# Linear attention into an MLP mixer: the first batch's steps in another order, with other PSUM banks

## The chip, the cores and the metric

The kernel runs on one core of a Trainium2 chip. The metric is device microseconds (us) of one execution. The kernel before took 245.57 us, the median of three runs (244.58 to 246.3). Lower is better.

## The reference

Inputs are q, k and v in float32, each of 8 batches x 8 heads x 576 positions x 64, and four weight matrices. Per batch:

```
phi(x) = where(x > 0, x, exp(x) - 1) + 1
kv  = phi(k)^T v                 # 64 x 64 per head
z   = sum over positions of phi(k)
x   = (phi(q) kv) / (phi(q) z + 1e-6)      # 576 x 512, heads side by side
u   = x + (relu(x^T w_tok1) w_tok2)^T      # token mixing, 576 -> 256 -> 576
out = u + relu(u w_ch1) w_ch2              # channel mixing, 512 -> 1536 -> 512
```

The output is 8 x 576 x 512 in float32.

## The kernel before

Matmuls run in bfloat16 and gather in float32 in PSUM, which has eight banks of 128 x 512. The 576 positions of a batch are cut into four full row blocks of 128 and a half one of 64 (the code's R = 4 and the index r = R); two batches share one block of tails. The eight batches go through the same stages, overlapped: loads, phi, kv, numerators and denominators, token mixing, channel mixing. Batches 1 to 7 do the channel mixing's products by a Winograd scheme with weight sums in place; batch 0 multiplies plainly.

**Order by hand.** Every step of the kernel is a named token (`put(name, fn)`), and the string `ORDER` lists all 1085 tokens; line 1167 emits them in that sequence. Each engine runs its own instructions strictly in that sequence, so `ORDER` is the queue of TensorE (PE), VectorE (DVE), ScalarE (ACT), GpSimd (POOL) and of the loads on SyncE (SP) at once. `BANK` gives each PSUM tile its bank by name, `EBUF` gives each exponential one of three SBUF buffers. A step waits for whoever wrote its inputs and for whoever still reads the bank or buffer it overwrites.

**The names that matter.** The leading digit is the batch. Batch 0's attention and token mixing are the tokens `A0` to `A43`, in the list `first` (line 1144):

- `A0`, `A4`, `A8`, `A16`: exponentials of k and q, in halves c = 0 and 1, on ACT (line 252); `A1`, `A5`, `A9`, `A17` (line 256) and `A3`, `A6`, `A11`, `A21` (line 262) finish phi on DVE.
- `A2`, `A14`, `A19`: `warm`, matmuls of zeros whose results nobody reads (line 1092).
- `A7`, `A15`: q turned by PE (line 320); `A10`, `A12`, `A18`, `A22`: the copies out of PSUM, on DVE or ACT (line 326).
- `A13`, `A25`: `ksum_first`, the sums z (line 564), with two small ACT copies (line 567). `A20`, `A26`: `kv_first` (line 573), with two ACT copies (line 577).
- `A23`, `A29`: denominators and numerators of a half (lines 588 and 595). `A24`, `A30`: reciprocals, `A27`, `A33`, `A35`: quotients, on DVE (lines 604 to 610). `A28`, `A31`: quotients of the half block, on ACT (line 619).
- `A32`, `A34`, `A36`, `A37`: `mm1_first`, the first token-mixing matmuls (line 627) with a relu on ACT (line 630). `A38`, `A39`, `A40`, `A43`: `mm2_first` (line 638), each with an add into u on DVE (line 640). `0gt`, `0gv`: the same for the half block (lines 653 and 658). `A41`, `A42`, `At2`, `At3`: u turned by PE (line 646) and copied out by ACT or DVE (line 648).

Then come, for batch 0, `0ma`/`0mb` 0 to 11: the first channel-mixing matmuls, in two halves of the contraction (line 686), with relus `0r` on ACT (line 695) or, for 3, 6 and 9, on DVE (line 693); and `0q0` to `0q11`, the second ones (line 747). For batch 1: loads `1L` (line 228), phi `1kx 1ka 1kb 1qx 1qa 1qb`, `1v0` (DVE) and `1v1` (ACT), which cast v (line 275), `1Q` and `1Qc` (lines 320, 326), `1K` and `1Kc` (lines 302, 308), numerators `1n` with `1nc` on DVE (lines 352, 361 to 364), `1f` with `1fr` on ACT (lines 448, 452), `1h` with `1hu` (lines 520, 523, 531, 533) and `1t` (line 538). `G..` are weight sums on DVE (line 897), `wt2` another (line 824), `ws..` weight sums on POOL (line 816). `B0` to `B2` load the last three quarters of w_ch2 (line 1126).

**Gates.** Three waits between transfers are written out: the load `1Lk0` waits until the first quarter of w_ch1 has landed, `B0` waits until the second half of batch 1's v (`1Lv1`) has landed, and `2Lq0` waits until the second quarter of w_ch2 (`B0`) has landed. The transfer `1Lq0`, half of batch 1's q, is issued fourth in SP's row of batch 1.

**The copies of w_tok2.** `w2_put` (line 664) sorts w_tok2's columns into `w2p`, which `mm2_first` reads: four copies, by kt = 0, 1 and by columns t = 0 to 3 and 4 to 8. They stand ahead of `ORDER`, all four on POOL.

Of the kernel before, what the change touches and what calls it, by code (L numbers as in the profile page):

```python
# [24 lines left out]

GSW = {2: 0, 1: 1, 0: 2}
# [15 lines left out]
BANK = {k_: int(v_) for k_, v_ in (e.split(":") for e in """2K:0 2n0:0 2n1:2 2n2:4 2f:6 2g0:3 2g1:6 2X2:5 2Z2:2 2Y2:1 2gt:6 3K:6 3n0:2 3n1:4 3n2:6 3f:3 3g0:6 3g1:6 3X2:2  # L42
3Z2:0 3Y2:5 3gt:4 4K:2 4n0:2 4n1:4 4n2:6 4f:6 4g0:4 4g1:0 4X2:2 4Z2:1 4Y2:3 4gt:6 5K:6 5n0:1 5n1:3 5n2:5 5f:5
5g0:5 5g1:3 5X2:4 5Z2:5 5Y2:7 5gt:1 6K:2 6n0:1 6n1:3 6n2:5 6f:2 6g0:5 6g1:2 6X2:4 6Z2:0 6Y2:6 6gt:6 7K:2 7n0:2
7n1:4 7n2:6 7f:2 7g0:0 7g1:2 7X2:3 7Z2:6 7Y2:1 7gt:5 2m2:0 2m3:1 2m4:2 2m5:3 2m8:1 2m9:1 2m10:0 2m11:1 3m2:0
3m3:1 3m4:2 3m5:3 3m8:1 3m9:0 3m10:0 3m11:1 4m2:0 4m3:1 4m4:2 4m5:3 4m8:1 4m9:1 4m10:0 4m11:1 5m2:0 5m3:1
5m4:2 5m5:3 5m8:1 5m9:0 5m10:0 5m11:1 6m2:0 6m3:1 6m4:2 6m5:3 6m8:1 6m9:1 6m10:0 6m11:1 1h00:7 1h01:6 1h10:5
1h11:6 1t0:7 1t1:0 1t2:1 1t3:6 1m0:2 1m1:0 1m2:0 1m3:4 1m4:5 1m5:6 1m6:6 1m7:2 1m8:5 1m9:7 1m10:1 1m11:6 T00:7
T10:3 T01:3 T11:0 T02:3 T12:7 U08:0 U18:3 7c0:3 7c1:4 7c2:4 7c3:6 7c4:2 7c5:4 7X0:5 7Z0:4 7Y0:1 7X1:2 7Z1:0
7Y1:0 7PX0:7 7PZ0:3 7PY0:1 7PX1:6 7PZ1:5 7PY1:5 7tX:0 7tZ:4 7tY:2 1PX:1 1PZ:2 1PY:5 2PX:0 2PZ:5 2PY:1 3PX:0  # L50
3PZ:3 3PY:4 4PX:7 4PZ:0 4PY:0 5PX:0 5PZ:7 5PY:1 6PX:7 6PZ:1 6PY:6 warm0:0 0Q00:1 0Q01:2 0s0:3 warm1:0 0Q10:1
0Q11:2 warm2:3 0K0:4 0d0:0 0n0:6 0l0:1 0s1:2 0K1:4 0d1:3 0n1:6 0l1:0 0f0:1 0f1:4 0g00:2 0g01:3 0g10:0 0t0:6
0t1:4 0g11:1 0m0:3 0m1:7 0t2:6 0t3:4 0m2:1 0m3:2 0gt:2 0m4:5 0m5:6 0m6:6 0m7:3 0m8:7 0m9:0 0m10:4 0m11:4 U00:1
U01:0 1Q0:4 U02:2 U03:3 1Q1:6 1K:4 1n00:6 1n01:6 1n10:4 1n11:4 1n20:4 1n21:6 1f:4 1g2:4 0ut:3 2X1:6 2Z1:4
2Y1:2 3X1:3 3Z1:5 3Y1:1 4X1:7 4Z1:0 4Y1:0 5X1:6 5Z1:0 5Y1:2 6X1:5 6Z1:6 6Y1:1 2X0:7 2Z0:3 2Y0:0 3X0:4 3Z0:0
3Y0:6 4X0:1 4Z0:7 4Y0:5 5X0:1 5Z0:5 5Y0:0 6X0:7 6Z0:3 6Y0:2""".split())}
# [3 lines left out]
EBUF = {k_: int(v_) for k_, v_ in (e.split(":") for e in """0k0:0 0q0:1 0q1:2 0k1:0 1k0:1 1k1:2 1q0:0 1q1:1 2q0:2 2q1:0 2k0:1 2k1:2 3q0:0 3q1:1 3k0:2 3k1:0 4q1:1 4q0:2  # L60
4k0:0 4k1:1 5k0:2 5k1:0 5q0:1 5q1:2 6k1:0 6k0:1 6q1:2 6q0:0 7k1:1 7k0:2 7q0:0 7q1:1""".split())}

YBUF = {k_: int(v_) for k_, v_ in (e.split(":") for e in """0k0:0 0q0:0 0q1:0 0k1:0 1k0:0 1k1:0 1q0:0 1q1:0 2q0:0 2q1:0 2k0:0 2k1:0 3q0:0 3q1:0 3k0:0 3k1:0 4q1:0 4q0:0
4k0:0 4k1:0 5k0:0 5k1:0 5q0:0 5q1:0 6k1:0 6k0:0 6q1:0 6q0:0 7k1:0 7k0:0 7q0:0 7q1:0""".split())}

ORDER = """A2 A0 A1 A3 A4 A5 A6 A8 A9 A7 A10 A12 A13 A14 A11 A16 A17 A15 A19 A18 A21 A20 A22 A23 A24 A25 A26 A27 A28 A29
A30 A33 A31 A32 A35 A34 A36 A37 A38 1Lk0 A39 1Lk1 1Lv1 A40 1Lq0 A41 1Lq1 A42 1Lv0 A43 0ma0 At2 0ma1 At3 0ma3
0mb1 0mb0 0ma6 0r0 0mb3 0r1 1ka0 0ma7 1kx0 0ma2 0ma8 0mb6 1kb0 0mb2 0r3 0mb8 0mb7 0r6 0r8 0ma4 0r7 G21 0gt
1kx1 G22 0ma9 0gv 0ma10 0mb4 1ka1 0r2 0ma5 0r4 G11 0mb10 1kb1 0mb5 0r10 G23 0mb9 0r5 0ma11 0mb11 0r9 1qa0 1qx0
B0 0q0 B1 0r11 1qb0 B2 1qx1 1qa1 1Q00 1Q01 0q1 1Qc01 1v0 1Qc00 0q2 1qb1 1v1 1Q10 1Q11 1K 1Qc11 2Lq0 ws02 1Qc10  # L70
0q3 2Lq1 1Kc0 1Kc1 2Lv0 ws04 1n20 1n01 2Lk0 1nc20 0q4 2Lk1 1nc01 2Lv1 1n10 0q5 1nc10 1n00 0q6 1nc00 1n11 0q7
1nc11 2qx0 1n21 ws14 0q8 1nc21 1f0 2qx1 2qa0 1f1 wt2 3Lq0 G24 0q9 1fr1 2qb0 1fr0 0q10 2qa1 2v0 G12 1h01 2qb1
1h00 1hu01 2qT1 ws00 0q11 1hu00 0z1 2kx0 1h10 2qT0 ws10 0z0 1h11 1hu10 1t0 1hu11 1t1 3Lv0 ws24 1g2 1tc1 1tc0
1t2 3Lq1 1t3 1gu2 1ma9 1tc3 ws12 0z2 1ma1 1ma5 1tc2 1ma4 0z3 1mb1 2v1 0o1 1mb5 1r1 1ma7 2ka0 2kx1 1mb7 G01
3Lk0 1ma10 0o0 G03 3qx0 1mb4 2kb0 0ut 1ma2 2ka1 1r4 1mb10 wt0 3Lk1 1mb2 1r7 1ma3 3Lv1 1r2 2kb1 1mb9 1r10 1ma8
3qa0 0uc 1mb8 1r5 ws20 1r9 2K 1r8 1mb3 2Kc0 2Kc1 3qb0 1ma6 1r3 2n ws30 2nd 1mb6 T00 2o0 ws34 1r6 2n1 1ma11
Tr00 2o1 ws22 1mb11 2ne 3v0 2n0 1ma0 1mb0 3qa1 T01 4Lv0 1r0 2n2 ws32 1r11 1p10 3qx1 2f0 1w13 G02 Tr01 4Lq1
1w10 1p11 3kx1 3qb1 1p20 3ka0 3kx0 2f1 1w20 G14 2fr0 4Lk0 T02 1w23 3qT1 1w30 1p50 Tr02 3kb0 1p51 2fr1 3qT0 1c0
1w40 1p21 4qx1 2g1 3ka1 1c2 1eZ 1p60 3v1 G13 1p61 2gu1 2g0 1c1 3kb1 2uT1 1p31 2gu0 4kx0 1p30 3K 4qa1 2uT0 1p71
3Kc1 1eY 3Kc0 4v0 1p70 4qb1 4Lv1 4Lq0 3n 1hY 1eW 4Lk1 U00 3ne 5Lv0 3nd 1hZ U01 3n2 U02 3o0 1hW 3n1 1p40 3n0  # L80
2x01 2x11 2s1 3o1 1p41 V0 2y11 2x02 2y01 2s2 1eX 2x15 2x21 2s3 1o 2x12 2y21 2x16 2y12 2x06 2y16 2s4 2x05 2y06
2y02 2x17 2y15 4qa0 2x26 4qx0 2x25 2y17 2x07 G04 3f0 2y25 4qb0 2y05 4ka0 2y26 4qT1 2x14 2x03 2y07 2y14 2x13
3fr0 4qT0 3f1 2y13 4kb0 2x27 5Lq0 3fr1 2y03 2x23 5Lk0 2x04 2y27 2x22 2y04 4ka1 2x24 4kx1 2y22 3gt 3g1 2y23
# [32 lines left out]
def kernel(  # L116
# [26 lines left out]
    R = 4  # L143
# [478 lines left out]
    def mm1_first(c, rs):  # L622
        ps = banks("0f1")[:, :, 0:DM // 2] if c else bank("0f0").rearrange("p (t c) -> p t c", t=NT)
        for mt in range(NT):
            ms = slice(128 * mt, 128 * mt + 128)
            for r in rs:
                nc.tensor.matmul(out=ps[:, mt], lhsT=w1t[:, 0, ms] if r == R else w1[:, r, ms],
                                 rhs=x[0][:, r, COLS[c]], start=(r == 0), stop=(r == R))
# [569 lines left out]
```

## Time and profile before

| | us |
|---|---|
| median of three runs | 245.57 |
| profiled execution, whole | 244.9 |
| its span, first to last instruction | 243.1 |
| PE busy | 232.1 (95%) |
| DVE busy | 211.6 (87%) |
| ACT busy | 136.4 (56%) |
| POOL busy | 80.6 (33%) |

The profile shows one execution of the program; times within it count from the start of its span. PE, DVE, ACT and POOL are the four computing engines; SPq is the queue of loads. A row of the timeline gives start, length, engine, line, operation, output<-input, shape, a count of merged instructions, and in brackets the idle time of the engine in front of it with what ended it. A row of the stages table gives, for a stretch of the span, its length and then each engine's busy time with its number of instructions, the granted TensorE clock (PEclk, 1.00 is full) and the share of the DMA engines' time.

### The profile page before, as it was taken

What the parts mean: (1) busy time and instruction counts of PE and PEld (TensorE: products, weight loads), DVE (VectorE), ACT (ScalarE), POOL (GpSimd) and SP (SyncE); (2) the same over time, 40 slices, a digit from 0 to 9 for tenths busy, and PEclk for the clock granted to TensorE, in tenths of its full rate; (3) what the DMA queues carried; (4) which work ended last, traced back from release to release, by engine and by line L of the source; (5) the groups of instructions that cost most, each with busy time, mean ns of one, the idle gap of its engine ahead of it and who ended that gap; (6) DMA issues with size and microseconds to landing.
All of it is one profiled execution on the core that took longest, in us unless ns stands there. A gap on an engine that the chain in (4) does not pass through costs nothing.

```text
span 243.1 us, 6362 instructions
## 1 busy us (share of the span) xinstructions
PE 232.1 (95%) x2597; PEld 173.9 (72%) x2616; DVE 211.6 (87%) x387; ACT 136.4 (56%) x224; POOL 80.6 (33%) x88
## 2 busy tenths in 40 slices
PE   7799989999999999999999999999999999999991
PEld 3485436465677686789877887788678867888881
DVE  5955896999999989999999999999999599867661
ACT  4773692759788277327994397448923442347000
POOL 8770035076900620035100620206014910440730
PEclk9999999999999999999999999999999999999997
DMA  6999999979779989969948979494791285143036
GB/s 240 270 203 249 340 286 295 411 204 368 272 237 197 266 257 162 260 76 308 291 125 173 377 254 199 85 299 138 162 138 36 44 175 109 24 94 79 3 82 178
DMA packets 49805, 48.42 MB, mean 199 GB/s; under 512 B 30064, under 2 KB 35568, under 8 KB 49776
## 3 DMA queue, kind: packets, MB, share of 16 engines
q1 hardware_dynamic: 41664, 35.00, 49.2%
q0 software_dynamic: 7472, 12.22, 25.4%
q10 hardware_dynamic: 640, 0.79, 1.0%
q8 instruction: 20, 0.33, 0.6%
q14 instruction: 9, 0.07, 0.1%
HBM read 35.85 MB, written 9.44 MB: 186 GB/s over the span
## 4 chain that ended last, share of the span: by engine, by line
PE 83%; DMA 9%; POOL 3%; issue 1%; SPq 1%; DVE 0%; ACT 0%; POOLq 0%; ACTq 0%
PE ps L970 27%; PE ps L928 23%; PE ps L747 6%; PE ps L448 6%; DMA q_raw<-in_q_dram 5%; PE ps L459 4%; PE ps L686 4%; DMA wc<-in_moe_w_ch_dram 4%; PE ps L711 2%; PE ps L733 2%; PE ps L302 2%; PE ps L1024 2%; PE ps L387 2%; POOL qT L1111 1%; PE ps L523 1%; PE ps L478 1%
## 5 line engine op out<-in xcount | busy, mean ns | idle before, releaser
L970 PE MATMUL ps<-k_raw,v_raw 128*128 128x256 bf16 x252 | 31.8, 273 | 0.0
L943 ACT COPY v_raw<-ps 128x512 f32<-128x512 f32 x30 | 17.0, 595 | 22.8 <-PE ps L928 21.5
L970 PEld LDWEIGHTS <-cr 128*128 128x128 bf16 x252 | 24.4, 98 | 4.8
L970 PEld LDWEIGHTS <-v_raw 128*128 128x128 bf16 x252 | 24.0, 98 | 3.8 <-issue 0.4
L928 PEld LDWEIGHTS <-swc 128*128 128x128 bf16 x240 | 23.4, 98 | 3.1
L681 DVE CUSTOM_DVE_ANT_0 cr<-ps,v_raw 128x512 bf16<-128x512 f32 x30 | 20.1, 683 | 4.5 <-PE ps L928 2.5
L928 PEld LDWEIGHTS <-wc 128*128 128x128 bf16 x216 | 21.1, 98 | 3.6
L928 PE MATMUL ps<-crt,swc 128*128 128x256 bf16 x180 | 23.1, 273 | 0.0
L686 PE MATMUL ps<-uT,wc 128*128 128x512 bf16 x91 | 21.8, 379 | 0.4 <-issue 0.2
L252 ACT ACTIVATE e<-q_raw 128x1152 bf16<-128x1152 f32 x16 | 18.7, 1166 | 5.9 <-DVE den L361 4.4
L970 PE MATMUL ps<-wc,cr 128*128 128x256 bf16 x168 | 21.6, 273 | 0.0
L1071 POOL TENSOR_TENSOR obuf<-obuf,w 128x512 f32<-128x512 f32 x6 | 8.2, 1359 | 38.6 <-ACT w L1058 19.5
L252 ACT ACTIVATE e<-k_raw 128x1152 bf16<-128x1152 f32 x16 | 18.5, 1166 | 3.7 <-DMA k_raw<-in_k_dram 3.0
L1071 POOL TENSOR_TENSOR obuf<-obuf,q_raw 128x512 f32<-128x512 f32 x6 | 8.2, 1372 | 35.6 <-DVE obuf L1064 35.6
L928 PE MATMUL ps<-uT,wc 128*128 128x256 bf16 x144 | 19.5, 273 | 0.0
L1064 DVE TENSOR_TENSOR obuf<-ps,u 128x512 f32<-128x512 f32 x24 | 16.4, 683 | 2.5 <-PE ps L970 2.4
L413 DVE TENSOR_TENSOR x<-ps,dens 128x768 bf16<-128x768 f32 x18 | 16.6, 929 | 0.0
L1071 POOL TENSOR_TENSOR obuf<-obuf,part 128x512 f32<-128x512 f32 x6 | 7.7, 1284 | 26.6 <-DVE dens L400 18.5
L686 PEld LDWEIGHTS <-wc 128*128 128x128 bf16 x96 | 8.9, 98 | 10.1 <-issue 0.9
L470 DVE TENSOR_TENSOR u<-ps,x 128x1024 bf16<-128x1024 f32 x12 | 14.5, 1217 | 0.2
L256 DVE TENSOR_SCALAR y<-k_raw 128x1152 bf16<-128x1152 f32 x16 | 12.0, 753 | 3.0 <-DMA k_raw<-in_k_dram 2.8
L836 DVE TENSOR_TENSOR v_raw<-cr 128x512 bf16<-128x512 bf16 (+3 forms) x24 | 14.4, 618 | 0.0
(168 smaller groups left out, 513.6 us busy)
## 6 DMA issues: line engine op xcount, KB each, us to landing
k_raw<-in_k_dram SPq DMA_DIRECT2D x16, 576.0 KB, 6.6
q_raw<-in_q_dram SPq DMA_DIRECT2D x16, 576.0 KB, 5.7
v_raw<-in_v_dram SPq DMA_DIRECT2D x14, 576.0 KB, 7.3
out_dram<-obuf POOLq DMA_DIRECT2D x12, 512.0 KB, 5.9
wc<-in_moe_w_ch_dram POOLq DMA_DIRECT2D x8, 384.0 KB, 10.3
out_dram<-obuf POOLq DMA_DIRECT2D x4, 256.0 KB, 6.0
cr<-in_v_dram POOLq DMA_DIRECT2D x2, 288.0 KB, 7.3
out_dram<-obuf POOLq DMA_DIRECT2D x4, 128.0 KB, 4.8
```

Source lines behind the costliest of these rows:

```text
L252: nc.scalar.activation(out=ebuf[EBUF[f"{n}{nm}{c}"]], in_=f, func=AF.Exp)
L413: nc.vector.tensor_tensor(out=xv[:, :, rc0:rc0 + 3], in0=nd_tile(n, m)[:, :, k0:k0 + 6, 0:D].rearrange("p i (q a) d -> p i q a d", a=2), i ...
L448: nc.tensor.matmul(out=banks(f"{n}f")[:, mt], lhsT=w1t[:, b, ms] if r == R else w1[:, r, ms], rhs=x[b][:, r, :], start=(r == 0), stop=(r = ...
L470: nc.vector.tensor_tensor(out=u[b][:, rs], in0=banks(f"{n}g{i}"), in1=x[b][:, rs], op=ALU.add)
L681: nc.vector._custom_dve(TENSOR_ADD_SAT, out=o, in0=ps, in1=c, s0=3.4028234663852886e38, s1=0.0)
L686: nc.tensor.matmul(out=bank(f"{n}m{mc}"), lhsT=wc1[:, kj, 128 * mc:128 * mc + 128], rhs=uTj[b][:, kj] if n < 2 - U1 else uT[b][:, :, kj], ...
L747: nc.tensor.matmul(out=bank(f"U{p}{t}"), lhsT=crt[:, kc, :] if t == 8 else cr[b][:, kc, 128 * r:128 * r + 128], rhs=wc2[:, kc, :], start=( ...
L928: nc.tensor.matmul(out=ps[:, j], lhsT=lhs[:, k_, 128 * j:128 * (j + 1)], rhs=rhs[:, :, k_], start=(first and j == 0 and k_ == 0), stop=(k_ ...
L943: nc.scalar.copy(out={1: c1, 6: c6, 5: c5}[i], in_=ps)
L970: nc.tensor.matmul(out=ps, lhsT=lhs[:, k_], rhs=rhs[:, k_], start=(first and not skip and k_ == 0), stop=(k_ == KH - 1), skip_group_check= ...
L1064: nc.vector.tensor_tensor(out=slots(f"{n}P", 4)[:, d::2, HC[c]], in0=pair_tile(n, "X" if z == "W" else z), in1=u[n % 2][:, d::2, HC[c]], o ...
L1071: nc.gpsimd.tensor_tensor(out=o, in0=o, in1=part[i], op=ALU.add)
```

## The change

The first 184 tokens of `ORDER`, up to batch 1's step `1h10` and the two transfers `2qT1` and `2qT0`, become 189 in another sequence; the 901 tokens from `1t0` on are the same as before. In detail:

- The sequence of all engines over these steps is redrawn, and so are the banks of the PSUM tiles in them. Behind them four tiles lie in other banks (those of the steps 1m3, 1m4, 1m8 and `0ut`), and 43 bank entries that no step uses are dropped.
- `A32` (`mm1_first` of half 0) becomes two tokens: `A32` does row blocks 0 to 3 of output block 0, `A32l` the half row block of output block 0, then all of output block 1 and the relu. The matmuls are the same.
- The four `w2_put` copies become tokens `Aw00`, `Aw11` (POOL) and `Aw01`, `Aw10` (DVE) inside `ORDER`.
- `warm` 2 and 1 (`A19`, `A14`) move up, directly behind `warm` 0; on ACT the small copies of `A13` now stand ahead of the exponential `A8`.
- `0gt` moves from the middle of the `0ma`/`0mb` steps to between `A41` and `A42`; all four `mm2_first` adds stand ahead of the copies `A42` and `At3` on DVE.
- The order of `0ma`/`0mb` becomes 5, 2, 7, 4, 8, 1, 6, 0, 10, 11, 9, 3 by their first halves, with the DVE relus `0r6`, `0r3`, `0r9` last. `0q1`, `0q0` and `0q2` now all stand ahead of `1Q01`. On DVE `1qb1` comes ahead of `1v0`; on ACT `1v1` comes ahead of `1qx0`, where it stood behind `1Qc00`.
- Six `EBUF` entries change: 0q1, 1q0, 1k0, 1k1, 2k0 and 3q0.

The order of the loads on SP, of `B0` to `B2` on POOL and the gates stay as they are.

```diff
-    def mm1_first(c, rs):
+    def mm1_first(c, rs, mts=range(NT)):
...
-        for mt in range(NT):
+        for mt in mts:
             ms = slice(128 * mt, 128 * mt + 128)
-            for r in rs:
+            for r in rs if c or mt == 0 else range(R + 1):
...
-    def w2_put(kt, t0, t1):
-        nc.gpsimd.tensor_copy(
+    def w2_put(kt, t0, t1, engine):
+        engine.tensor_copy(
...
-    for t0, t1 in ((0, 4), (4, T)):
+    for i, (t0, t1) in enumerate(((0, 4), (4, T))):
         for kt in range(NT):
-            w2_put(kt, t0, t1)
+            put(f"Aw{i}{kt}", w2_put, kt, t0, t1, (nc.gpsimd, nc.vector)[(i + kt) % 2 if W2V == 1 else 0])
...
-             lambda: den_first(1), lambda: num_last(1), lambda: mm1_first(0, range(R1)),
+             lambda: den_first(1), lambda: num_last(1), lambda: mm1_first(0, range(R), [0]),
...
+    put("A32l", mm1_first, 0, [R])
```

The redrawn part of `ORDER`, old and new:

```diff
-A2 A0 A1 A3 A4 A5 A6 A8 A9 A7 A10 A12 A13 A14 A11 A16 A17 A15 A19 A18 A21 A20 A22 A23 A24 A25 A26 A27 A28 A29
-A30 A33 A31 A32 A35 A34 A36 A37 A38 1Lk0 A39 1Lk1 1Lv1 A40 1Lq0 A41 1Lq1 A42 1Lv0 A43 0ma0 At2 0ma1 At3 0ma3
-0mb1 0mb0 0ma6 0r0 0mb3 0r1 1ka0 0ma7 1kx0 0ma2 0ma8 0mb6 1kb0 0mb2 0r3 0mb8 0mb7 0r6 0r8 0ma4 0r7 G21 0gt
-1kx1 G22 0ma9 0gv 0ma10 0mb4 1ka1 0r2 0ma5 0r4 G11 0mb10 1kb1 0mb5 0r10 G23 0mb9 0r5 0ma11 0mb11 0r9 1qa0 1qx0
-B0 0q0 B1 0r11 1qb0 B2 1qx1 1qa1 1Q00 1Q01 0q1 1Qc01 1v0 1Qc00 0q2 1qb1 1v1 1Q10 1Q11 1K 1Qc11 2Lq0 ws02 1Qc10
-0q3 2Lq1 1Kc0 1Kc1 2Lv0 ws04 1n20 1n01 2Lk0 1nc20 0q4 2Lk1 1nc01 2Lv1 1n10 0q5 1nc10 1n00 0q6 1nc00 1n11 0q7
-1nc11 2qx0 1n21 ws14 0q8 1nc21 1f0 2qx1 2qa0 1f1 wt2 3Lq0 G24 0q9 1fr1 2qb0 1fr0 0q10 2qa1 2v0 G12 1h01 2qb1
-1h00 1hu01 2qT1 ws00 0q11 1hu00 0z1 2kx0 1h10 2qT0 ws10 0z0 1h11 1hu10
+A2 A0 A1 A3 A4 A5 A6 A19 A14 A13 A8 A7 A12 A9 A10 A11 A16 A15 A22 A17 A21 A20 A25 A23 A18 A26 A29 1Lk0 A24 A27 A30 A33
+A28 A32 A35 Aw01 A31 Aw10 A32l A34 A36 Aw00 A37 A38 Aw11 A39 A43 A40 A41 0gt A42 At3 At2 0ma5 0ma2 0mb5 0r5 1Lk1 1Lv1
+0ma7 0ma4 0ma8 0mb7 0r7 0mb8 0mb2 0gv 1ka0 1Lq0 0ma1 1Lq1 1kx0 1Lv0 0mb1 0r1 1kb0 0ma6 0mb4 G21 0ma0 G23 0r2 0mb0 B0
+B1 0r8 0ma10 B2 0r4 2Lq0 G11 0r0 0mb10 0r10 1kx1 0ma11 0mb11 0mb6 0ma9 G22 2Lq1 G12 0ma3 0mb3 0r11 0mb9 G24 0q1 1ka1
+0r6 1kb1 0r3 1v1 2Lv0 0r9 0q0 0q2 1qa0 1qx0 1qb0 1Q01 2Lk0 1qx1 1qa1 ws04 1Qc01 1Q00 1qb1 1Qc00 1v0 1Q11 1Qc11 2Lk1
+1Q10 1K 1Kc0 1Qc10 1Kc1 0q3 1n01 1nc01 2qx0 1n20 1nc20 0q4 0q5 2qx1 1n10 0q6 ws02 1nc10 1n11 1nc11 ws14 2v0 0q7 1n00
+1nc00 0q8 0q9 2qa0 1n21 1nc21 2qb0 2Lv1 3Lq0 2qa1 0q10 1f0 wt2 1fr0 1f1 2qb1 ws00 0q11 0z0 1fr1 1h01 1hu01 1h00 2kx0
+1h11 0z1 1hu00 1h10 1hu10 2qT1 2qT0 ws10
```

## The prediction

> **What bounds it.** I read the page's engine shares first, then the slices, then the chain that ended last, then busy time by stage.
>
> ```profile
> PE 232.1 (95%) x2597; PEld 173.9 (72%) x2616; DVE 211.6 (87%) x387; ACT 136.4 (56%) x224; POOL 80.6 (33%) x88
> ...
> PE   7799989999999999999999999999999999999991
> ...
> PE 83%; DMA 9%; POOL 3%; issue 1%; SPq 1%; DVE 0%; ACT 0%; POOLq 0%; ACTq 0%
> ```
>
> PE is full from the seventh slice on; what it lacks lies in the first six (37 us), all of it inside the redrawn part. By stage:
>
> ```profile
> core 0: us, PE busy (x) PEld busy (x) DVE busy (x) ACT busy (x) POOL busy (x), PEclk, DMA share, GB/s
> 0.00:20.00 20.00, 16.09 (x204) 10.93 (x205) 14.25 (x29) 11.98 (x27) 14.82 (x25) 1.00 1.07 235
> 20.00:32.16 12.16, 11.96 (x60) 5.36 (x60) 8.23 (x16) 7.45 (x12) 0.96 (x2) 1.00 1.13 324
> 32.16:37.80 5.64, 4.79 (x104) 2.77 (x103) 4.65 (x8) 4.93 (x6) 1.96 (x3) 1.00 1.12 227
> 37.80:51.22 13.42, 13.32 (x92) 7.62 (x87) 11.69 (x29) 6.96 (x10) 4.71 (x5) 1.00 1.00 347
> 51.22:243.10 191.88, 185.94 (x2151) 147.22 (x2163) 172.78 (x308) 105.07 (x171) 58.16 (x56) 0.99 0.68 176
> ```
>
> From 37.80 (`0q3`) to 51.22 (`1t0`) PE is busy but for 0.10 us, and the same steps fill that stretch after the change; behind it the order is the same. So the forecast is one question: when does `0q3` start, 37.80 before? Up to 20 us latency rules (loads, exponentials, quotients); from 20 to 32 the first channel-mixing matmuls of batch 0 fill PE; in 32.16 to 37.80 the chain shows who is late:
>
> ```profile
> 8.10 9.93 DMA wc<-in_moe_w_ch_dram
> ...
> 19.48 12.67 DMA q_raw<-in_q_dram
> ...
> 32.24 1.17 ACT e L252
> ...
> 33.44 0.77 DVE qp L262
> ...
> 34.25 0.68 PE ps L320 x9
> ```
>
> The first quarter of w_ch1 lets the loads of batch 1 go; its q lands at 32.16, and PE stands about 1.0 us (33.24 to 34.25) until phi is made. The DMA share is above 1 until there: transfers are the pace, and the change alters neither their order nor their gates, so I keep every landing.
>
> **The prologue, costed at nothing.** The two warm steps (rows 1.11 and 0.65, but 0.216 us from start to start, six of them: 1.3) now follow the first, which frees PE at 6.7; so the z sums run at 8.0 instead of 8.7, and ACT takes their copies ahead of `A8`:
>
> ```profile
> 7.84 1.16 ACT L252 ACTIVATE e<-q_raw 128x1152 bf16<-128x1152 f32 x1 [0.82 <-DMA q_raw<-in_q_dram]
> 8.99 0.58 ACT L326 COPY qT<-ps 128x512 bf16<-128x512 bf16 x1
> 9.48 0.34 ACT L567 CAST kvbd<-ps 64x2 bf16<-64x2 f32 x2
> 9.83 1.16 ACT L252 ACTIVATE e<-k_raw 128x1152 bf16<-128x1152 f32 x1
> ```
>
> In these rows `A8` starts at 7.84; now z is ready at 8.4, the copies end at 8.8, `A8` runs 8.8 to 9.95, `A12` to 10.5, `A16` to 11.7 (before 11.0). phi(k) of half 1 ends at 12.5 (11.9), and PE does `A25` ahead of `A23`, so the numerators of half 0 come at 13.1 (12.30), their quotients (1.22) end at 15.0 (14.18), the other half's two (1.29) at 16.8 (16.06). That is 0.7 late. It is won back: `mm1_first` waited until 15.29 for ACT's half-block quotients, which shared a bank with its output; with that bank apart and `A32` split it can run at 15.4, its 20 matmuls at 0.108 end at 17.5, and the first add into u starts at 17.5+0.43+0.27 = 18.2, before 18.18. Bounds: 0.4 earlier (numerators not late) to 0.6 later (the full slip). I take 0, since both sums end within 0.05.
>
> The two weight copies on DVE stand between 16.8 and the add at 18.2. No row shows such a copy on DVE; POOL's four took 2.65 (0.66 each), DVE's memset of 260 elements 0.28. Two cost 0.6 to 1.3: cover is 1.4, and the second must be done for a matmul at 17.95, so the dear end adds 0.2. I take 0, near DVE's own row. The dropped POOL copies free nothing: POOL then idles 13 us.
>
> **Turning u, worth 0.5.** Before, from the add at 18.18, PE had four 128x512 matmuls (0.86) done when its dense run began at 22.02, so the run counts from 21.16; later `0gt` interrupts it and costs 0.65 (27.45 to 28.31, less one pitch). Now four adds (0.63 each) end 2.5 after the first, `At3`, `At2` follow, and the run begins 3.1 after it, at 21.3, with `0gt` already done in a wait. 21.16+0.65-21.3 = 0.5. Its 48 matmuls at 0.216 end at 31.7 (32.16), and with `0q1`, `0q0`, `0q2` (12 matmuls, 2.6; w_ch2's first quarter lands at 31.3) PE is covered until 34.26: the 1.0 us hole is filled.
>
> **The q chain, where the gain is collected.** ACT after `0r7` (24.5): two exponentials of k, seven relus at 0.5, `1v1` 1.17 add up to about 32.1; q lands at 32.16, so `1qx0` keeps 32.24 to 33.4 with 0.1 to spare. DVE: `0r3` and `0r9` now come last, bound by PE's end at 31.7: `0r9` ends at 32.7, `1qa0` (0.76) at 33.4, `1qb0` 33.46 to 34.2 (33.44 before): no cover is left. `1Q01` starts at 34.3. Then:
>
> ```profile
> 33.44 0.76 DVE L262 TENSOR_TENSOR qp<-e,y 128x1152 bf16<-128x1152 bf16 x1 [0.16 <-ACT e L252]
> 34.23 0.76 DVE L256 TENSOR_SCALAR y<-q_raw 128x1152 bf16<-128x1152 f32 x1
> 34.99 0.77 DVE L275 CAST vs<-v_raw 128x1152 bf16<-128x1152 f32 x1
> 35.67 0.75 DVE L262 TENSOR_TENSOR qp<-e,y 128x1152 bf16<-128x1152 bf16 x1
> ```
>
> The last two change places: `1qb1` ends at 35.7 instead of 36.4, and `1Q11`, `1Q10` follow at 35.8 to 36.3, behind a new hole of about 1.0 on PE (34.8 to 35.8), since `0q1` and `0q2` are used up. `1K` waits for `1v0` (36.45) and runs 36.5 to 37.2; `1v1` is long done (before, it ended at 37.20). `0q3` starts at 37.2 instead of 37.8. So the hole moves more than it goes, and 0.6 is left. `0q3` can't start before 36.94, when the second quarter of w_ch2 lands.
>
> **From 37.2 on.** I walked the numerators, `1f`, `1h`: v of batch 2 lands at 45.7, ACT casts it until 46.9 ahead of `1fr0`, the second relu ends at 48.35 for `1h01` at 48.4; `1hu00` ends at 50.4 for `1t0` at 50.6. No gain, no loss, but three margins of 0.1 to 0.2: I charge 0.1. Splitting `mm1_first` and other banks add no instruction. Two exponentials of batch 3 now share a buffer: its first reader ends at 62.46, the second writer started at 67.00, so that is free.
>
> **Sum.** -0.6+0.1 = -0.5 on the profiled execution: 244.9 to 244.4 (span 243.1 to 242.6). The median of the runs lies 0.67 above that execution; on it I forecast 245.57-0.5 = 245.1. One per cent, 2.5 us, is about what a measurement of this kernel can tell from no change.
>
> **The rivals.**
>
> *Given back by DVE* (chance 0.22): from `0r9` to `1K` nothing covers any more, so each 0.1 that the prologue or the copies slip is 0.1 of gain lost; at 0.6, the bound above, the time is 245.6. For it: ACT's slip of 0.7. Against: PE's split wins it back.
>
> *The clock falls* (0.22; the other side): with the warm steps gone from 8.96 and 10.59, PE has no matmul from about 8.8 to 10.8 and again from 11.8 to 12.5. The end of the trace shows what a pause can do:
>
> ```profile
> 237.02:238.20 1.18, 1.15 (x11) 0.76 (x8) 0.70 (x2) 0.00 (x0) 0.00 (x0) 1.00 0.91 253
> 238.20:240.40 2.20, 0.00 (x0) 0.00 (x0) 0.42 (x1) 0.00 (x0) 0.00 (x0) 1.00 0.90 276
> 240.50:243.10 2.60, 0.00 (x0) 0.00 (x0) 0.00 (x0) 0.00 (x0) 0.00 (x0) 0.50 0.20 58
> ```
>
> The granted clock halved 2.2 us after the last matmul. At the start the warm matmuls took 0.85 from start to start, and 0.43 after about 3.5 us of work. Decision point: a fall at 10.8 to 11.8. Then the matmuls between 12.5 and 15.2 (about 1 us of streaming) take double, `0q3` comes 0.9 later than forecast, +0.3 over before: 245.9. If the return takes 3.5 us of dense work more, another 1.7 is added: +2.0, 247.6. Against: 2.1 us of pause is just short of 2.2, and the pause isn't alone in its stretch.
>
> [...]
>
> *Up to the landing* (0.08): DVE and ACT hide, `0q3` at 37.0: 244.8.
>
> *Not what it says* (0.02): an unseen wait on a bank or buffer behind `1t0`; PE's 190 us there have no cover, so a wait of 0.5 shows in full: 245.6 or more.
>
> **Numbers.** Forecast 0.46; 245.1, its own range 244.5 to 245.7. The range reaches from 243.9 (the landing limit, less 0.9 for medians that spread from 244.58 to 246.3) to 247.4, just short of the clock's longer form. Faster by over 1% needs `0q3` 1.7 us before its weights land: 0.04. Slower by over 1%: the clock's longer form with spread, 0.09, and unseen waits of that size, 0.05: 0.14. Within: 0.82.
>
> **What would show it.** Right: `0q3` (line 747 behind line 302) at 37.2, `0gt` before the dense run, line 686 ending at 31.7, a PE hole before the second turn of line 320. Wrong: matmuls of 128 columns at 0.11 from start to start around 13 us (clock), `A8` not at 8.8, DVE's line 262 for q later than 33.5, or landings that moved.

## The result, and the profile after

The kernel after took 248.03 us, the median of six runs (246.84 to 250.51), beside 245.03 for six runs of the kernel before on the same chip: a ratio of 1.0126, with a 95% interval of 1.0089 to 1.0164. The forecast was 245.1, its range ended at 247.4. The change made the kernel slower by 1.3%. (Ratios leave out single runs over 1.5% above the fastest of their kernel; below this matters in one experiment, and is said there.)

The profiled execution took 248.08 us, its span is 246.3 (before 244.9 and 243.1). Lines of the code behind the string `ORDER` have moved up by four: line 682 is the old 686, 743 the old 747, 316 the old 320. First the page of the kernel after, shares and slices:

```profile
PE 235.7 (96%) x2616; PEld 176.1 (72%) x2616; DVE 213.7 (87%) x389; ACT 136.5 (55%) x224; POOL 81.2 (33%) x86
...
PE   7689996999999999999999999999999999999992
...
PEclk9958999999999999999999999999999999999999
...
PE 93%; DVE 3%; issue 1%; ACT 1%; DVEq 0%
```

PE is busy 3.6 us longer, though its matmuls are the same. Not all of this is the change: before's trace has 19 matmul records fewer (2597 and 2616), and behind `1t0`, where the steps are the same, PE's busy time differs by 1.15 us all the same (187.09 and 185.94 in the stages). The PEclk line shows what is new: in the third slice the granted clock is 0.5, in the fourth 0.8. Before, it was full there. DMA, 9% of the old chain, is gone from the chain: the loads no longer set the pace. The stages, cut at the same steps as before (start of the last matmul of the first dense run, `0q3`, `1t0`), in the columns of the earlier table:

```profile
0.00:20.00 20.00, 15.79 (x176) 10.63 (x177) 13.62 (x28) 10.97 (x25) 14.09 (x23) 0.83 1.07 233
20.00:34.61 14.61, 14.54 (x89) 7.89 (x88) 9.34 (x19) 9.34 (x16) 2.70 (x3) 1.00 1.11 316
34.61:41.47 6.86, 4.93 (x105) 2.85 (x103) 6.57 (x10) 3.87 (x5) 3.12 (x2) 1.00 1.19 257
41.47:54.84 13.37, 13.37 (x95) 7.64 (x88) 11.29 (x27) 7.12 (x9) 3.25 (x4) 1.00 0.72 264
54.84:246.30 191.46, 187.09 (x2166) 147.13 (x2163) 172.88 (x308) 105.19 (x171) 58.09 (x56) 1.00 0.69 177
```

The last matmul of the first dense run starts at 34.61 (before 32.16), `0q3` starts at 41.47 (37.80), `1t0` at 54.84 (51.22). Behind `1t0` nothing is lost: 191.46 against 191.88. So 2.45 us were lost before the end of the dense run and 1.2 more between it and `0q3`. The chain that ended last has both places; from it four pieces (start, length, what):

```profile
9.47 0.18 ACT e L248
...
17.40 3.52 PE ps L623 x20
...
24.63 8.65 PE ps L682 x40
...
39.07 1.64 DVE vs L271
```

`A8`, which stood at 7.84 and was forecast for 8.8, starts at 9.47. The 20 matmuls of `mm1_first` last 3.52 us where the forecast had 20 x 0.108, about 2.2. And DVE's cast of v (`1v0`), 0.77 before, is on the path with 1.64. Reading the clock by stretches of 3.41 us gives the first of the two losses (it changed at 6.36, 13.18, 20.01 and 245.29 in this record, at 4.91 and 240.43 in before's: 6.82, 6.83, 225.28 and 235.52 apart, which is 2, 2, 66 and 69 times 3.413):

```profile
6.36:9.77 3.41, 3.24 (x27) 2.14 (x25) 2.75 (x5) 1.79 (x4) 3.41 (x5) 1.00 1.10 324
9.77:13.18 3.41, 1.11 (x46) 0.90 (x47) 2.56 (x5) 3.37 (x6) 1.83 (x3) 1.00 1.30 197
13.18:16.59 3.41, 3.13 (x80) 2.80 (x81) 2.37 (x6) 1.32 (x8) 2.83 (x5) 0.50 1.28 203
16.59:20.01 3.42, 3.42 (x22) 2.61 (x21) 2.23 (x4) 1.85 (x8) 0.28 (x1) 0.50 1.32 204
```

PE is busy only 1.11 us of the second stretch, and behind it the clock is halved for two stretches. What left PE so empty is in PE's timeline:

```profile
8.94 0.66 PE L316 MATMUL ps<-identity,qp 128*128 128x128 bf16 x9
11.48 0.68 PE L316 MATMUL ps<-identity,qp 128*128 128x128 bf16 x9 [1.88 <-DVE qp L258]
12.09 0.48 PE L569 MATMUL ps<-cr,kp 64*64 64x64 bf16 x36
13.15 0.40 PE L560 MATMUL ps<-ones,kp 128*128 128x2 bf16 x9 [0.59 <-DVE kp L258]
```

Between the two turnings of q PE waits 1.88 us for phi(q). Before, the two warm steps `A14` and `A19` stood in such pauses.

### The profile page after: what moved, and what is told of

Read it like the earlier page. It is cut to its first block, busy times and chain, and to the rows that moved or that the text cites. A ratio compares the mean times of both kernels' runs of the same rounds, so it can differ in the third digit from the quotient of the medians.

```text
span 246.3 us, 6376 instructions
## 1 busy us (share of the span) xinstructions
PE 235.7 (96%) x2616; PEld 176.1 (72%) x2616; DVE 213.7 (87%) x389; ACT 136.5 (55%) x224; POOL 81.2 (33%) x86
## 4 chain that ended last, share of the span: by engine, by line
PE 93%; DVE 3%; issue 1%; ACT 1%; DVEq 0%
PE ps L966 26%; PE ps L924 22%; PE ps L682 8%; PE ps L444 6%; PE ps L743 5%; PE ps L455 4%; PE ps L1088 3%; PE ps L707 2%; PE ps L729 2%; PE ps L298 2%; PE ps L1020 2%; PE ps L383 2%; PE ps L623 1%; PE ps L591 1%; PE ps L634 1%
## 5 line engine op out<-in xcount | busy, mean ns | idle before, releaser
L966 PE MATMUL ps<-wc,cr 128*128 128x256 bf16 x168 | 21.6, 273 | 0.0
L258 DVE TENSOR_TENSOR kp<-e,y 128x1152 bf16<-128x1152 bf16 x16 | 12.0, 751 | 3.7 <-ACT e L248 3.6
```

The lines of the kernel that those rows point to most:

```text
L966: nc.tensor.matmul(out=ps, lhsT=lhs[:, k_], rhs=rhs[:, k_], start=(first and not skip and k_ == 0), stop=(k_ == KH - 1), skip_group_check= ...
```

## The experiments

All ratios are to the kernel before on the same chip, with 95% intervals.

### The warm steps back in their pauses

Only two tokens of the kernel after move: `A14` behind the first turning of q, `A19` behind the second.

```diff
-A2 A0 A1 A3 A4 A5 A6 A19 A14 A13 A8 A7 A12 A9 A10 A11 A16 A15 A22
+A2 A0 A1 A3 A4 A5 A6 A13 A8 A7 A14 A12 A9 A10 A11 A16 A15 A19 A22
```

> The changed kernel with its two short warm steps put back to their old places on TensorE, one behind each turning of batch 0's q; all else as changed. If the clock alone made the change slow: full granted clock from about 6 us to the end, the first add into u at 17.5 to 18.2 us (21.5 in the changed kernel), step 0q3 at 37.0 to 37.4, and a time 0.3 to 0.8 us below the kernel before. If the new order itself costs (ScalarE's later start, VectorE without cover): full clock, but 0q3 at 38 us or later and a time at or over the kernel before. If the places of the warm steps don't matter: the clock falls again and the time stays 3 us over.

It took 244.33 us (243.62 to 245.16, 12 runs), ratio 0.9975 [0.996, 0.999]: faster than both kernels. The mean granted clock was 0.997 or more in all 12 runs. Its stages, cut at the same steps:

```profile
0.00:20.00 20.00, 17.28 (x204) 11.45 (x204) 15.50 (x32) 12.06 (x27) 13.83 (x23) 1.00 1.08 237
20.00:31.38 11.38, 11.35 (x62) 5.39 (x62) 7.76 (x16) 8.48 (x14) 0.46 (x1) 1.00 1.13 325
31.38:37.06 5.68, 4.70 (x103) 2.75 (x102) 5.40 (x9) 3.86 (x5) 2.21 (x4) 1.00 1.09 243
37.06:50.59 13.53, 13.53 (x95) 7.65 (x87) 11.39 (x27) 7.02 (x9) 5.22 (x5) 1.00 1.06 349
```

(The second stage ends here with the first `0q`, one matmul later than above.) The clock is full, `0q3` starts at 37.06 and `1t0` at 50.59. So the redrawn order is worth what the forecast said, and 4.41 us of `0q3`'s place in the kernel after (41.47 less 37.06) hang on where two steps of dead matmuls stand. PE's timeline has the warm steps (line 1088) between the turnings:

```profile
8.29 0.68 PE L316 MATMUL ps<-identity,qp 128*128 128x128 bf16 x9 [0.17 <-DVE qp L258]
8.80 1.08 PE L1088 MATMUL ps<-v_raw 128*128 128x256 f32 x4
10.53 0.68 PE L316 MATMUL ps<-identity,qp 128*128 128x128 bf16 x9 [0.65 <-DVE qp L258]
11.04 0.65 PE L1088 MATMUL ps<-v_raw 128*128 128x256 f32 x2
```

### The opposite: the kernel before with the warm steps moved up

```diff
-A2 A0 A1 A3 A4 A5 A6 A8 A9 A7 A10 A12 A13 A14 A11 A16 A17 A15 A19 A18
+A2 A19 A14 A0 A1 A3 A4 A5 A6 A8 A9 A7 A10 A12 A13 A11 A16 A17 A15 A18
```

> The kernel before with only its two short warm steps moved up, directly behind the long one. Clock theory: the granted clock falls to a half between 10 and 15 us and returns 3.4 to 7 us later; 1.5 to 3.5 us slower than the kernel before. Order theory: within 0.5 us of the kernel before, since the two steps only leave two gaps on TensorE that others ended anyway.

It took 246.28 us (244.46 to 247.46, 10 runs), ratio 1.0046 [1.0025, 1.0068]. The runs form two groups: six with a mean clock of 0.984 to 0.986 took 246.24 to 247.46, four with 0.996 to 0.998 took 244.46 to 245.51. The profiled one belongs to the second group, so no trace shows the first. In the old order the moved steps cost 1.5 us over the kernel before when the lower clock appears (the median of the six is 246.46, of the four 245.19), the low end of what was expected of a fall, and it doesn't always appear. In the profiled run the thinnest stretch of 3.41 us, 10.05 to 13.47, has a streamed share of 0.42 by the count of the last section, where the kernel after has 0.21.

### No warm steps at all

The kernel after without `A19` and `A14`: three float32 matmuls of 256 columns, six rows in the profile, whose results nobody reads, are left out.

```diff
-A2 A0 A1 A3 A4 A5 A6 A19 A14 A13 A8
+A2 A0 A1 A3 A4 A5 A6 A13 A8
```

> The changed kernel without its two short warm steps, whose results nobody reads. Clock theory: the gap on TensorE is as before or longer, so the clock falls as in the changed kernel, and the time is within 0.7 us of it (the sums z come 1.3 us sooner, so ScalarE is no longer late; that may win 0.3 to 0.7). Order theory, in which the slip of 0.7 us on ScalarE is what hurts: at least 1.5 us faster than the changed kernel.

248.0 us (246.71 to 249.66, 4 runs), ratio 1.0128 [1.0092, 1.0165]: as slow as the kernel after. `A8` starts at 8.29, 1.18 earlier than there, since nothing stands ahead of the z sums on PE. Most of that arrives: the first add into u is at 20.54 (21.46 there), `0q3` at 40.69 (41.47). But the clock fell twice in this record, and the second fall takes it back: `1t0` is at 55.43 (54.84). These are the two stretches ahead of the falls:

```profile
9.54:12.96 3.42, 2.14 (x73) 1.96 (x74) 2.90 (x6) 2.84 (x7) 1.54 (x3) 1.00 1.31 199
36.85:40.27 3.42, 1.48 (x68) 1.14 (x69) 3.31 (x5) 1.18 (x2) 2.84 (x2) 1.00 1.22 225
```

PE was busy 2.14 of 3.42 us in the first, and the clock fell all the same. The kernel after, with 1.75 busy from 37.07 to 40.49, kept it. Busy time is not what decides.

### One warm step back, and the other

`A14` alone (two float32 matmuls, four rows in the profile) or `A19` alone (one, two rows) stands behind the first turning of q; the other stays in front.

```diff
-A2 A0 A1 A3 A4 A5 A6 A19 A14 A13 A8 A7 A12
+A2 A0 A1 A3 A4 A5 A6 A19 A13 A8 A7 A14 A12     (four rows back)
+A2 A0 A1 A3 A4 A5 A6 A14 A13 A8 A7 A19 A12     (two rows back)
```

> The changed kernel with only the longer of the two short warm steps (A14, four passes, 0.86 us) put back behind the first turning of q. By the traces so far the clock fell in stretches of 3.41 us in which the array streamed for 0.35 of the time or less, and stayed at 0.37 or more; the changed kernel's worst stretch had 0.21, this adds 0.25. Clock theory: full clock in all runs, 0q3 at 37.0 to 37.4 us, a time within 0.3 us of the one with both steps back (0.3 to 0.9 under the kernel before). If both steps are needed, or their places and not their work: the clock falls, 1.5 to 3.5 us over.

> The changed kernel with only the shorter of the two short warm steps (A19, two passes, 0.43 us) put back behind the first turning of q. It adds 0.13 to the worst stretch's 0.21, so 0.34, just under where the traces so far put the border. Clock theory: the clock falls in some or most runs, and the runs fall into two groups 2 to 4 us apart by their mean granted clock (0.984 and 0.996 or more). If any matmul in the gap is enough: full clock in all runs.

Four rows back: seven of ten runs had a clock of 0.991 or more and took 243.79 to 246.38; three had 0.975 or 0.976 and took 249.04 to 249.58. The ratio of the seven is 0.9995 [0.9971, 1.0019]. The profiled run is one of the three: its clock fell at 13.88, and again at 41.19. Two rows back: 249.52 (249.15 to 250.27, 4 runs), ratio 1.0195 [1.0161, 1.023], clock 0.974 or 0.975 in every run. So two rows are too little, four hold it in most runs, and both steps (the first experiment) in all. A full clock in all runs had been expected of the four rows, and of the two a fall in some or most.

### Is it work in the pause, or streaming?

The kernel after, with extra matmuls behind the first turning of q, unread: 40 of 2 columns, or 28 of 128 columns.

```diff
-A2 A0 A1 A3 A4 A5 A6 A19 A14 A13 A8 A7 A12
+A2 A0 A1 A3 A4 A5 A6 A19 A14 A13 A8 A7 Ax A12
+    def narrow(m, cols):
+        ps = bank("warm1")
+        for _ in range(m):
+            nc.tensor.matmul(out=ps[:, 0:cols], lhsT=identity, rhs=(ones if cols == 2 else identity)[:, 0:cols],
+                             start=True, stop=True)
+    put("Ax", narrow, 40, 2)      # the other kernel: 28, 128
```

> The kernel after, with 40 extra matmuls of 2 columns (identity against ones, result unread) behind the first turning of q, in the pause where the kernel after has PE idle from 9.43 to 11.48. They make PE busy in that pause but stream only 80 columns, some 0.03 us of the array at 0.216 us for 512 columns. If the clock is granted by how much the array streams in a window of 3.4 us: it falls as in the kernel after (half near 13, first add into u at 21.3 to 21.6 and not at 18.0), time 2.5 to 4.5 us over the kernel before. If any work on PE in the pause holds the clock: full clock, first add at 18.0 to 18.3, time 0.2 to 0.9 under the kernel before.

> The kernel after, with 28 extra matmuls of 128 columns (identity against identity, result unread) at the same place: 28 x 128 columns at 512 in 0.216 us are 1.5 us of streaming in the pause. Both theories (streamed share of a window, any work on PE) expect the clock to hold: full from about 7 on, first add into u at 18.0 to 18.3, time 0.2 to 0.9 under the kernel before in all runs. If instead the order of the kernel after costs something of its own that the moved warm matmuls only hid, the time stays 1 us or more over the kernel before with a full clock.

The narrow ones: 249.36 us (248.67 to 251.13, 4 runs), ratio 1.0179 [1.0128, 1.0231], clock 0.972 to 0.981. Their stretch ahead of the fall and the one behind it:

```profile
8.51:11.92 3.41, 2.51 (x94) 2.22 (x91) 2.62 (x5) 3.35 (x6) 2.35 (x3) 1.00 1.25 204
11.92:15.33 3.41, 2.76 (x79) 2.43 (x76) 2.57 (x6) 1.33 (x7) 2.11 (x4) 0.50 1.30 204
```

PE was busy 2.51 of 3.41 us, with no idle time over 0.90 us in PE's timeline, and the clock was halved:

```profile
8.81 1.14 PE L1158 MATMUL ps<-ones,identity 128*128 128x2 bf16 x40
10.85 0.68 PE L316 MATMUL ps<-identity,qp 128*128 128x128 bf16 x9 [0.90 <-DVE qp L258]
```

The first add into u is at 20.53 (21.3 to 21.6 expected; `A8` starts 0.63 earlier than in the kernel after). The wide ones: 245.06 us (244.53 to 247.95, 10 runs), ratio 1.0032 [0.9994, 1.007]. The profiled execution has a full clock and its first add at 18.51:

```profile
8.95:12.36 3.41, 2.89 (x78) 2.50 (x75) 2.54 (x5) 3.36 (x6) 2.15 (x3) 1.00 1.28 200
```

That a busy PE holds the clock is refuted by the narrow fill; that streaming holds it fits both. Two of the ten runs with the wide fill had a clock of 0.981 and 0.982 and took 247.84 and 247.95; where they lost it no trace shows, so the expectation that all runs keep it was missed. The median stayed near the kernel before and not 0.2 to 0.9 under it. A part of this shows in the profiled run: `A8` starts at 9.06 here instead of 8.52, and the first add is about as much later than in the first experiment (18.51, 18.02).

### The cast of v beside POOL's sums

`ws04`, sums of weights on POOL (line 812), waits for `1v0`'s cast, and `ws02` stands behind it on POOL; nothing else of the kernel after changes.

```diff
-1qa1 ws04 1Qc01 1Q00 1qb1 1Qc00 1v0 1Q11
+1qa1 1Qc01 1Q00 1qb1 1Qc00 1v0 ws04 1Q11
-        copy(out=vs[:, js, :, 0:D],
+        live["cast", n, c] = copy(out=vs[:, js, :, 0:D],
-        first = {(0, 0): ("phi", "q", 2, 1), (2, 0): ("phi", "k", 2, 1)}.get((i, k0))
+        first = {(0, 0): ("phi", "q", 2, 1), (0, 4): ("cast", 1, 0), (2, 0): ("phi", "k", 2, 1)}.get((i, k0))
```

> The changed kernel, its warm steps left up, but GpSimd's first two weight sums (ws04, ws02) wait until VectorE has cast 1v0. In the changed kernel that cast took 1.72 us beside those sums, 0.77 in the kernel before, and TensorE waited for it. If the sums slow the cast: the clock still falls, the cast takes 0.75 to 0.80 us, step 0q3 comes 0.9 to 1.0 us sooner after the first add into u (20.0 to 19.0 us), and the time is 0.6 to 1.0 us under the changed kernel, so 2.0 to 2.5 over the kernel before. If the cast is slow for another reason (the half clock, the transfers): it still takes 1.7 us and the time stays.

247.57 us (247.0 to 247.82, 4 runs), ratio 1.0107 [1.0078, 1.0135]. The timelines of DVE and POOL in the kernel after:

```profile
38.31 0.76 DVE L258 TENSOR_TENSOR qp<-e,y 128x1152 bf16<-128x1152 bf16 x1
38.99 1.72 DVE L271 CAST vs<-v_raw 128x1152 bf16<-128x1152 f32 x1
...
38.35 3.36 POOL L812 TENSOR_TENSOR q_raw<-wc 128x512 f32<-128x512 bf16 x2 [4.55 <-DVE y L252]
```

and with the sums behind the cast:

```profile
38.89 0.76 DVE L271 CAST vs<-v_raw 128x1152 bf16<-128x1152 f32 x1
...
39.79 2.26 POOL L812 TENSOR_TENSOR q_raw<-wc 128x512 f32<-128x512 bf16 x2 [6.09 <-DVE vs L271]
```

The cast takes 0.76 again and two sums 2.26 instead of 3.36; the way from the first add into u to `0q3` is 19.05 us (21.36 to 40.41) where it was 20.01. The clock fell here too, at 13.05, so only this loss is gone. The median doesn't resolve it: 0.6 to 1.0 us under the kernel after was expected, and the two ratios, 1.0107 and 1.0126, lie within each other's intervals. In the kernel after the cast lost 0.96 and the two sums 1.10: the first sum, started at 38.35 beside DVE's product for phi(q) (from 38.31), ends at 40.08, the cast at 40.71, the second sum at 41.71. That is the price of this one meeting; by what the two hinder each other no run shows.

### The step on the q chain alone

The kernel before with `1qb1` ahead of `1v0`, `0q1` ahead of the first turning of batch 1, and `1v1` ahead of `1qx0`, as the kernel after has them.

```diff
-1qa0 1qx0 B0 0q0 B1 0r11 1qb0 B2 1qx1 1qa1 1Q00 1Q01 0q1 1Qc01 1v0 1Qc00 0q2 1qb1 1v1 1Q10
+1qa0 1v1 1qx0 B0 0q0 0q1 B1 0r11 1qb0 B2 1qx1 1qa1 1Q00 1Q01 1Qc01 1qb1 1v0 1Qc00 0q2 1Q10
```

> The kernel before with three moves of the change alone: 0q1 ahead of the turning of batch 1's q on TensorE, 1qb1 ahead of 1v0 on VectorE, 1v1 ahead of 1qx0 on ScalarE. The prediction's step on the q chain: 0q3 at 37.0 to 37.2 instead of 37.8 us, 0.5 to 0.8 us faster, full clock. If that step was wrong (a cast of v that is late, or contention on VectorE): 0q3 at 37.8 or later and no gain.

245.02 us (244.51 to 245.58, 12 runs), ratio 1.0005 [0.9995, 1.0014]: no difference. Two of its rows on PE show why (its line 317 is 320 of before):

```profile
34.80 0.68 PE L317 MATMUL ps<-identity,qp 128*128 128x128 bf16 x9 [0.62 <-DVE qp L259]
...
36.46 0.68 PE L317 MATMUL ps<-identity,qp 128*128 128x128 bf16 x9
```

The first turning comes 0.55 later than before (34.25), because `1v1` now stands ahead of `1qx0` on ACT and lets it start at 32.78 instead of 32.24; the second is at 36.46 (36.49 before), and `0q3` at 37.84 (37.80). The expected gain didn't come. In the first experiment ACT is free earlier (`1v1` at 30.58 instead of 31.73), and there the same step starts `1qx0` at 31.89; that the earlier dense run is what frees ACT is read from the order of the steps, not tested alone.

### The old first batch with the new rest

The kernel after with `A0` to `A29` in the old sequence.

```diff
-A2 A0 A1 A3 A4 A5 A6 A19 A14 A13 A8 A7 A12 A9 A10 A11 A16 A15 A22 A17 A21 A20 A25 A23 A18 A26 A29 1Lk0 A24 A27 A30 A33
+A2 A0 A1 A3 A4 A5 A6 A8 A9 A7 A10 A12 A13 A14 A11 A16 A17 A15 A19 A18 A21 A20 A22 A23 A24 A25 A26 A27 A28 A29 1Lk0 A30 A33
```

> The new order, but batch 0's steps up to the numerators of half 1 (A0 to A29) in the old sequence, so with the warm steps in the gaps, the z copies behind A8 on ScalarE and the numerators of half 0 ahead of A25 on TensorE. The prediction's step on the prologue says that ScalarE's slip of 0.7 us is won back: then the first add into u comes 0.3 to 0.7 us sooner than with the warm steps alone put back (18.02), at 17.3 to 17.7, and yet 0q3 stays at 36.8 to 37.2, held by the landings of q and w_ch2, and the time is within 0.4 us of that kernel. If the slip costs: 0q3 below 36.8 and 0.5 us or more faster than that kernel.

244.81 us (243.89 to 246.67, 12 runs), ratio 1.0003 [0.998, 1.0027]. The first add into u is at 18.01, no earlier than with the new sequence and the warm steps in place (18.02), though v's second half landed 1.0 later in this record (12.67, 11.68), so the comparison is weak; 0.3 to 0.7 earlier was expected, and a time within 0.4 us of the first experiment's (the two ratios are 0.0028 apart, 0.7 us). Its clock fell once in the profiled run, in the hole of the new q chain:

```profile
33.51:36.92 3.41, 1.54 (x17) 0.86 (x16) 3.17 (x5) 2.74 (x4) 0.00 (x0) 1.00 1.21 209
36.92:40.33 3.41, 3.41 (x84) 2.07 (x82) 1.18 (x3) 0.75 (x2) 2.34 (x2) 0.50 1.19 257
```

`0q3` came at 38.67. The hole was wider here: batch 1's first k landed at 26.27 (24.66 in the first experiment), and the first turning came at 35.01 (34.02). So the hole that the change opens before the second turning can also cost the clock, if a stretch of 3.41 us lies badly over it.

## Why the prediction was wrong

*What failed: the prologue, costed at nothing.* Its step "won back" holds only at a full clock. From the start of `A8` to the first add into u it takes, by kernel:

| kernel | `A8` | first add | between | granted clock there |
|---|---|---|---|---|
| before | 7.84 | 18.18 | 10.34 | full |
| after | 9.47 | 21.46 | 11.99 | half 13.18 to 20.01 |
| no warm steps | 8.29 | 20.54 | 12.25 | half 12.96 to 19.79 |
| 40 narrow matmuls | 8.84 | 20.53 | 11.69 | half 11.92 to 18.75 |
| warm steps back | 8.52 | 18.02 | 9.50 | full |
| 28 wide matmuls | 9.06 | 18.51 | 9.45 | full |

At a full clock the new order needs 0.84 less than the old one, and the forecast's 18.2 lies between the two kernels that kept it (18.02 and 18.51). At half the clock it needs 2.2 to 2.75 more than that. A second, smaller miss of the same step: it had the z sums at 8.0 and `A8` at 8.8. With both warm steps in front of them on PE (in the chain, line 1088 lasts 7.41 us from 1.46, against 6.45 with `A2` alone) the sums ran at 8.71 and `A8` at 9.47. That is 0.95 more than with the steps back, and it passes through: with the wide fill `A8` is 0.54 later and the add 0.49. How late `A8` is goes with when the clock first rises: with both steps in front it starts at 8.84, 9.06, 9.40 and 9.47 where the clock rose at 5.09 (narrow), 5.54 (wide), 6.22 (sums wait) and 6.36 (after). In before's record, from which the forecast worked, it rose at 4.91. (There the warm rows of 512 columns start 0.85 us apart from 2.47 to 4.18, and 0.43 from 4.98 on.)

*The clock falls* was thus the case that came, at 0.22. Its long form priced the clock well: 0.9 and 1.7 of delay, where 2.49 was measured. That its 247.6 lies so near 248.03 is partly luck: it meant 2.0 over the kernel before, whose median fell from 245.57 to 245.03 with three more runs, and 3.0 was measured. Three things in it were wrong. The point of decision was a pause of 2.2 us, read from the end of the trace, and the first pause (1.88 in PE's timeline, forecast 2.1) was called just short; the clock fell after it all the same, and with no idle time over 0.90 us in its stretch (narrow fill). The fall at the end of before's trace, at 240.43, had this stretch of 3.41 us ahead of it, with a streamed share of about 0.3 by the count of the last section:

```profile
237.02:240.43 3.41, 1.15 (x11) 0.76 (x8) 1.13 (x3) 0.00 (x0) 0.00 (x0) 1.00 0.91 270
```

By that count the 2.2 us between the last matmul and the fall say only where the stretch ended. Second, the range stopped just under the long form; yet in all ten profiled falls ahead of the end the clock was lost for whole stretches of 3.41 us, one in the four of the q chain (36.92 to 40.33 in the old first batch), two in the six of the first batch (13.18 to 20.01 in the kernel after). Third, a fall was not taken to upset what comes behind it.

*The q chain* was right in form and lost 0.96 at a place that no step named. With the clock full, everything is where it was forecast: the run of `0ma` ends at about 31.4 (31.7), PE has its hole of 1.0 us before the second turning (0.98), `0q3` starts at 37.06 (37.2). With the clock fallen, phi(q) of half 1 ends at 39.07, and by then the second quarter of w_ch2 has landed (36.88) and POOL starts its sums at 38.35, beside the cast; in the first experiment the cast is over (36.30) when they start (36.82), and so it was before. The losses add up: 0.95 for the later `A8`, 2.49 for the clock and 0.96 for the cast and 0.01 of rest make the 4.41 between the two kernels at `0q3`.

*Turning u, worth 0.5*, held: the dense run begins 3.0 us after the first add in both (18.02 to 21.02, 21.46 to 24.46), forecast 3.1. *The two weight copies on DVE* took 1.03 together, 0.52 each, inside the 0.28 to 0.66 given for each, and were covered. *The landings* stayed: q of batch 1 at 31.97 (32.16). (ACT's work ahead of it, "about 32.1", comes to 31.5 by the forecast's own terms; in the first experiment `1v1` ended at 31.74, so the margin was there.) *From 37.2 on*: 13.53 us from `0q3` to `1t0` with a full clock, 0.11 more than before (13.42), as charged.

*The sum*, -0.5, was right for the order alone: the first experiment is 0.25% faster, 0.6 us of 245. *Given back by DVE* and *Up to the landing* did not come about; the change did what it says, so *Not what it says* falls too.

One run of the kernel after took 250.51 with a mean clock of 0.975. The kernels with such a mean, where they were profiled (no warm steps, two rows back, four rows back), fell twice, the second time near 40 in the q chain's hole. That this run did the same is likely and not shown.

## What to carry to other kernels

A step whose result nobody reads can hold the clock, as the two warm steps did here (ratio 0.9975 with them in the pauses, 1.0126 with them moved up): before moving such matmuls, estimate from the trace's rows what PE would stream in each stretch (3.41 us by this clock's changes), not how long it idles (the clock fell in the narrow fill, with no idle time over 0.90 us). Place the filler in the thinnest stretch; too much ahead of it delays the chain, as the late `A8` shows (9.47 against 8.52). And price a lost clock with what it makes meet later: here a delay of 3.4 us set a DVE cast beside POOL's sums, which cost another microsecond (0.96).

## What the runs showed of the hardware

**In these records the clock went with what PE streamed.** Count for each stretch of 3.41 us the columns that the matmuls stream, at 0.216 us for 512 columns in bfloat16 (four of before's line 747 take 0.86 in the chain, from 39.26) or 256 in float32 (the warm rows of 256 columns in the kernel after start 0.216 apart, at 7.41, 7.63 and 7.84), times the share of 128 x 128 weights that each holds (128\*128 or 64\*64 in the rows). In the kernel after from 9.77 to 13.18 these are nine turnings of 128 columns (0.49) and 36 matmuls of 64 columns with a quarter of the weights (36 x 0.027 / 4 = 0.24): 0.73 us, a share of 0.21. This is an estimate, worked out from the matmul rows (a matmul across an edge moves a share by a few hundredths at most):

| kernel | stretch | PE busy, us | streamed share | clock behind it |
|---|---|---|---|---|
| after | 9.77 to 13.18 | 1.11 | 0.21 | half |
| two rows back | 9.37 to 12.78 | 1.67 | 0.26 | half |
| 40 narrow matmuls | 8.51 to 11.92 | 2.51 | 0.31 | half |
| no warm steps | 36.85 to 40.27 | 1.48 | 0.30 | half |
| old first batch | 33.51 to 36.92 | 1.54 | 0.34 | half |
| no warm steps | 9.54 to 12.96 | 2.14 | 0.35 | half |
| four rows back | 10.47 to 13.88 | 2.15 | 0.38 | half |
| q chain alone | 11.25 to 14.66 | 2.86 | 0.37 | full |
| after | 37.07 to 40.49 | 1.75 | 0.39 | full |
| before | 11.74 to 15.15 | 2.78 | 0.39 | full |
| warm steps back | 10.45 to 13.87 | 3.24 | 0.57 | full |
| 28 wide matmuls | 8.95 to 12.36 | 2.89 | 0.68 | full |

In these rows the border lies near 0.37 by this estimate, and PE's busy time does not sort them. Counted over all stretches at a full clock in the twelve records, none above 0.38 has a fall behind it, and none under 0.37 is without one. The kernel before stood just above the border (0.39). Where the stretches begin differs from record to record (the clock first rises between 4.42 and 7.05), which would explain why some orders lose the clock in some runs only; no pair of traces of one kernel shows it. The weighting by the share of the weights is inferred, and no run changed it alone; without it the rows do not sort (no warm steps from 36.85 would have 0.61 and fell, the kernel after from 37.07 has 0.39 and stayed).

**Getting it back goes by the same count.** At half the clock PE streams half as many columns in the same time (four matmuls of line 623 from 17.20 to 18.05 in the kernel after, from 15.13 to 15.56 in the first experiment). In columns, the six stretches behind a fall that did not bring the clock back have a share of 0.24 to 0.37 (13.18 to 16.59 in the kernel after: about 0.31, with PE busy 3.13 us), the ten that did 0.46 to 0.51. The same border fits; by it, a stretch at half the clock would have to be more than about three quarters full (0.37 of 0.5).

**A cast of 128 x 1152 from float32 on DVE took 1.72 instead of 0.76** beside two-input sums on POOL, which took 3.36 instead of 2.26 for two. It took 1.71 or 1.72 in all five records in which they met (after, no warm steps, 40 narrow matmuls, four and two rows back).
